# Attention scores by products over 64 rows and 72 keys, two heads side by side on the array, from keys kept unmasked in two copies

## The chip, the cores and the metric

The kernel runs on one core of one Trainium2 chip. The metric is the device time of one execution in microseconds (us). Of the kernel before there are three runs, with a median of 1661.16 us (1660.9 to 1661.81).

The engines of the core are called by the profile's names: PE (TensorE, matmuls), PEld (TensorE's weight loads, which the profile lists apart), DVE (VectorE), ACT (ScalarE), POOL (GpSimd) and SP (SyncE, which here issues most of the DMA transfers).

## The reference

Pooled attention is followed by two feed-forward layers. The change is in the attention, in the first product below.

```python
# q, k, v: (8, 8, 576, 64) f32
pool = 8
k_p = k.reshape(B, H, 72, pool, D).mean(axis=3)
v_p = v.reshape(B, H, 72, pool, D).mean(axis=3)
scores = 1 / sqrt(64) * q @ k_p^T            # (8, 8, 576, 72)
attn = exp(scores - max(scores)); attn /= attn.sum() + 1e-9
x = attn @ v_p                               # as 4608 tokens of 512
x = relu(x @ w_in) ** 2 @ w_out              # 512 -> 2048 -> 512
out = leaky(x @ w2_in) @ w2_out              # 512 -> 2048 -> 512
```

## The kernel before, in words

**Stages.** The first stage does the attention and the first product of the first feed-forward layer, `x @ w_in`, and stores the squares `h1`. `Middle` and `Second` then do the rest, with large products alone. The attention of block 0 (tokens 0 to 511) stands in `start()` in an order written out by hand (`START`), that of block 1 in `second_attention()`, and that of blocks 2 to 8 in a planner: `FirstStage` describes each step as an operation with an engine, a duration in us, a rank and buffers, and `Plan.run` sorts them by the times at which they could start. The program gets that order, engine by engine, and each engine then runs its own list strictly in order.

**Attention by tiles.** A tile is 128 tokens (36 tiles in 9 blocks of 512). A batch has 576 tokens, so four of the 36 tiles (4, 13, 22 and 31) belong half to one batch and half to the next (`parts_of`): there are 40 parts. For a tile the steps are: load q; four transposes on PE (line 682) and a copy by ACT (line 691) give `qt`, in which a pair of heads lies on the 128 partitions, head 2c on rows 0 to 63 and head 2c+1 on rows 64 to 127; the score products (line 728); the maximum of each head by DVE (line 738); the exponentials by ACT, one instruction for each head (line 750); the division (lines 767 to 769); the transposes of the probabilities (lines 808, 816); and their split into a high and a low part (lines 822, 825).

**Keys.** For each batch the 576 pooled keys (8 heads of 72) lie on partitions in five chunks of 128, the last of 64. `k_mask_parts` multiplies each pooled key row by a mask of two columns (1 for even and 0 for odd heads, and the reverse, times the scale), so that a row of 64 numbers becomes 128, of which one half is zero (line 524). Transposed (lines 550 and 556) they are `kt`, 128 by 576. With the zeros in place one product over 128 rows gives the scores of a pair of heads: 128 tokens by 144 keys, the first 72 columns of head 2c, the others of head 2c+1.

**Score products.** `score_parts(i, hf)` does half of a tile, two such products into one bank of PSUM; the planner places the two halves of a tile apart, with other work between. Each product in f32 appears in the trace as two weight loads and two matmul instructions.

**Rounding.** The large products of the stage (line 1000) are in f32r, one instruction each.

Of the kernel before, what the change touches and what calls it, by code (L numbers as in the profile page):

```python
# [16 lines left out]
P = 128  # L17
# [6 lines left out]
C_ID, C_PAR, C_VM, C_RA, C_RB, C_RP, C_N = 16, 0, 10, 12, 13, 14, 144  # L24


def constants(sp, nk, scale):
    c = np.zeros((P, C_N), np.float32)
    c[:, C_ID : C_ID + P] = np.eye(P, dtype=np.float32)
    p = np.arange(P)  # L30
    for t in range(nk):
        for j in range(2):
            c[:, C_PAR + 2 * t + j] = ((t * P + p) // sp % 2 == j) * (scale / POOL)
# [10 lines left out]
def attention_relu2_leaky_kernel(  # L44
# [26 lines left out]
    BLOCKS = NT // T  # L71

# [350 lines left out]
    kps, kts, kms, vps, vrps, vst, qT, sc = {}, {}, {}, {}, {}, {}, {}, {}  # L423
# [26 lines left out]

    def k_pool_pe(b, n):

        full, tail = KEYS // P, KEYS % P
        if n == 0:
            kps[b] = sb([P, 512], F32, "qt")[:, : NK * D].rearrange("p (c d) -> p c d", d=D)
            k_sums.extend([acc_bank(0), acc_bank(1)])
        ps, last = k_sums
        for c in range(2) if n == 0 else range(2, full):
            halves(ps, c, raws[("k", b, c)], P)
        if n == 0:  # L460
            return None
        halves(last, 0, raws[("k", b, full)], tail)

        def rest():
            halves_sum(kps[b][:, :full], ps, 0, full)
            halves_sum(kps[b][:tail, full:], last, 0, 1)

        return rest

    def k_pool(b, c):  # L470
        raw = raws[("k", b, c)]
        n = min(P, KEYS - c * P)
        if c == 0:
            kps[b] = sb([P, 512], F32, "qt")[:, : NK * D].rearrange("p (c d) -> p c d", d=D)
        nc.vector.tensor_reduce(
            out=kps[b][:n, c, :],
            in_=raw[:n].rearrange("p (r d) -> p d r", r=POOL),
            op=ALU.add,
            axis=AX.X,
        )  # L480

    def pooled_by_halves(out, x, n):

        def halve(w):
            to = out if w == D else x[:n, :, :w]
            nc.vector.tensor_tensor(
                out=to, in0=x[:n, :, :w], in1=x[:n, :, w : 2 * w], op=ALU.add
            )

        return [lambda w=w: halve(w) for w in (4 * D, 2 * D, D)]  # L490

    def k_pool_rows(b):
        kps[b] = sb([P, NK * D], F32, "kp").rearrange("p (c d) -> p c d", d=D)
        return pooled_by_halves(kps[b][:, : KEYS // P], raws.pop(("k", b, "rows")), P)

    def k_pool_tail(b):
        n = KEYS % P
        pooled_sum(kps[b][:n, KEYS // P], raws.pop(("k", b, "tail"))[:n])
# [9 lines left out]
    def k_mask(b):  # L508

        for fn in k_mask_parts(b):  # L510
            fn()

    def k_mask_parts(b):
        full, tail = KEYS // P, KEYS % P
        kp = kps.pop(b)
        km = (home() if b == 0 else sb([P, 512], F32, "r" if b == 1 else "gh"))[:, : full * 2 * D]
        km = km.rearrange("p (c j d) -> p c j d", j=2, d=D)
        kt = sb([P, 2 * D + 8], F32, "km")[:, : 2 * D].rearrange("p (j d) -> p j d", j=2)
        par = cst[:, C_PAR : C_PAR + 2 * NK].rearrange("p (c j) -> p c j", j=2)
        kms[b] = km, kt  # L520

        def masked(out, c0, c1, n):
            shape = [n, c1 - c0, 2, D]
# [7 lines left out]
        return [  # L531
            lambda: masked(km, 0, full, P),
            lambda: masked(kt.unsqueeze(1), full, NK, tail),
        ]
# [5 lines left out]
    def k_transpose_parts(b):  # L540
        full, tail = KEYS // P, KEYS % P
        km, last = kms.pop(b)
        copy = nc.vector.tensor_copy if b > 1 else nc.scalar.copy
        ps = {}

        def rows():
            kts[b] = sb([P, KEYS], F32, "kt")
            ps[0] = bank()
            for c in range(full):
                nc.tensor.transpose(  # L550
                    ps[0][:, c * P : (c + 1) * P], km[:, c].rearrange("p j d -> p (j d)"), ident
                )

        def rest():
            ps[1] = bank()
            nc.tensor.transpose(
                ps[1][:, :tail], last[:tail].rearrange("p j d -> p (j d)"), ident[:tail, :tail]
            )
# [138 lines left out]
    def score_products(i):  # L697
        rest = []
        for hf in range(2):
            products, top, exps = score_parts(i, hf)  # L700
            products()
            rest.append(lambda top=top, exps=exps: (top(), exps()))
        return rest

    def score_parts(i, hf):
        at = {}

        def products():
            if hf == 0:
                if i in first_tiles:  # L710
                    if not first_s:
                        t = home_tile([P, 3, KEYS]).rearrange("p n (h k) -> p n h k", h=H)
                        first_s.extend(t[:, n] for n in range(3))
                    s = first_s.pop()
                else:
                    s = sb([P, H, SP], F32, "s")
                sc[i] = s, sb([P, H], F32, "l"), sb([P, H], F32, "m"), qT.pop(i)
            qt = sc[i][3]
            if i in first_tiles:
                ps = acc_bank((2 * i + hf) % KC)  # L720
            else:
                ps = acc_bank(KC - 1) if i < 2 * T // P and hf == 0 else bank()
            at["ps"] = ps
            for b, _, r0, n in reversed(parts_of(i)):
                for c2 in range(NP // 2):
                    cc = hf * (NP // 2) + c2
                    keys = slice(cc * PAIR, (cc + 1) * PAIR)
                    nc.tensor.matmul(
                        ps[: r0 + n, c2 * PAIR : (c2 + 1) * PAIR],
                        lhsT=qt[:, cc, : r0 + n],  # L730
                        rhs=kts[b][:, keys],
                        start=True,
                        stop=True,
                    )

        def top():
            m = sc[i][2]
            nc.vector.tensor_reduce(  # L738
                out=m[:, hf * HH : (hf + 1) * HH],
                in_=at["ps"][:, : HH * SP].rearrange("p (h k) -> p h k", h=HH),  # L740
# [5 lines left out]
        def exps():  # L746
            s, l, m, _ = sc[i]
            for h in range(HH):
                g = hf * HH + h
                nc.scalar.activation(  # L750
                    out=s[:, g, :],
                    in_=at["ps"][:, h * SP : (h + 1) * SP],
# [5 lines left out]
        return products, top, exps  # L758
# [144 lines left out]
    def start():  # L903

        t0, rest, exps = 0, {}, {}
        for word in START:
# [21 lines left out]
            elif x == "k":  # L928
                for c in range(NK):
                    k_pool(n, c)  # L930
                k_mask(n)
# [129 lines left out]
    def second_attention():  # L1061
# [5 lines left out]
        pe[0] += [pooled_late[0], lambda: k_mask(b)]  # L1067
# [175 lines left out]
    class FirstStage:  # L1243
# [20 lines left out]
        def add_keys(self, b, rank):  # L1264
            rows, tail, kp, km, kl, kt = (
                Buffer(t) for t in ("wo4", "raw", "kp", "gh", "km", "kt")
            )
# [7 lines left out]
            for n, us in enumerate((1.22, 0.69, 0.43)):  # L1275
# [6 lines left out]
            y = self.op("DVE", 1.03, lambda: k_pool_tail(b), rank, after=[load_tail, x], uses=[tail, kp])  # L1282
            masks = []

            def mask(n):
                if n == 0:
                    masks.extend(k_mask_parts(b))
                masks[n]()
# [11 lines left out]
            t0 = self.op("PE", 0.63, lambda: turn(0), rank, after=[x, y], gets=[p0, kt], uses=[km])  # L1300
            c0 = self.op("DVE", 0.69, lambda: turn(1), self.CHAIN, after=[t0], uses=[p0, kt])
            t1 = self.op("PE", 0.2, lambda: turn(2), rank, after=[y, t0], gets=[p1], uses=[kl])
# [59 lines left out]
        def add_attention(self, blk):  # L1362
# [9 lines left out]
            for i in tiles:  # L1372
# [22 lines left out]
                for hf in range(2):  # L1395
# [4 lines left out]
                    self.tile[i] = x  # L1400
                    for b, *_ in parts_of(i):
                        self.scored[b] = x
                    after = [x]
# [893 lines left out]
```

## Time and profile before

| | us |
|---|---|
| median of three runs | 1661.16 |
| the profiled execution | 1660.31 |
| its span, first to last instruction | 1658.5 |
| PE busy in it | 1618.0 |
| DVE busy | 1264.1 |
| ACT busy | 834.4 |

The profiled execution lies 0.85 us under the median, and 1.8 us of it lie outside the span. Busy time is the union of an engine's instructions; the matmuls of PE overlap (the next begins before the last has drained), so its busy time says that something was under way, not that the array worked at its peak.

### The profile page before, as it was taken

The page shows a single profiled execution, that of the slowest core. Times are in us where ns is not written, and L with a number is a line of the kernel's source. Part 1 is how long each engine was busy: PE and PEld are TensorE (multiplying, and loading weights), DVE is VectorE, ACT ScalarE, POOL GpSimd, SP SyncE. Part 2 cuts the span into 40 slices and gives each one's busy share as a digit, 9 for nine tenths or more (in the row PEclk, how much of TensorE's full clock was granted, in tenths as well). Part 3 has the DMA queues.
Part 4 walks back from the last instruction along what each step waited for, and adds up shares of the span by engine and source line. Part 5 has one row for each costly group of instructions (what it writes and reads, how often), then busy time and mean ns, then how long its engine had stood idle before and what let it go on. Part 6 is the DMA issues. An engine that isn't in the chain of part 4 may idle for free. (4 is left out here: it accounts for less than half of the span.)

```text
span 1658.5 us, 26685 instructions
## 1 busy us (share of the span) xinstructions
PE 1618.0 (98%) x9560; PEld 1470.8 (89%) x9560; DVE 1264.1 (76%) x2214; ACT 834.4 (50%) x1797; POOL 102.4 (6%) x191
## 2 busy tenths in 40 slices
PE   7999889999999999999999999999999999999998
PEld 6888768888888898888888899999999999999998
DVE  7967879887766678696879887877877866666665
ACT  6766657756754754343435544443445533333332
POOL 0121011121121200000000000000000000000000
PEclk9999999999999999999999999999999999999999
DMA  8827766776566977575757766557638754544443
GB/s 236 268 89 221 221 213 218 228 247 218 189 229 217 330 241 258 186 251 189 253 206 249 281 212 211 181 191 235 204 131 291 242 169 153 159 154 153 153 156 106
DMA packets 272325, 345.78 MB, mean 208 GB/s; under 512 B 55360, under 2 KB 201024, under 8 KB 272192
## 3 DMA queue, kind: packets, MB, share of 16 engines
q1 hardware_dynamic: 257152, 296.36, 55.6%
q0 software_dynamic: 14464, 47.20, 7.6%
q8 instruction: 75, 1.23, 0.3%
q10 hardware_dynamic: 576, 0.52, 0.1%
q14 instruction: 58, 0.48, 0.1%
HBM read 208.74 MB, written 135.27 MB: 207 GB/s over the span
## 5 line engine op out<-in xcount | busy, mean ns | idle before, releaser
L1000 PE MATMUL acc<-xh,wi 128*128 128x512 f32 x640 | 221.3, 403 | 0.1
L1000 PE MATMUL acc<-wo,wi 128*128 128x512 f32 x704 | 191.2, 399 | 1.7 <-ACT r L1011 1.7
L1000 PEld LDWEIGHTS acc<-wo,wi 128*128 128x128 f32 x704 | 129.1, 188 | 27.4 <-ACT r L1011 2.0
L1000 PEld LDWEIGHTS acc<-xh,wi 128*128 128x128 f32 x640 | 121.2, 190 | 24.2 <-ACT r L1011 0.5
L1000 PE MATMUL acc<-xl,wi 128*128 128x512 f32 x320 | 125.6, 393 | 0.0
L2181 PE MATMUL ps<-wi,hh 128*128 128x256 f32 x512 | 93.9, 283 | 0.0
L2181 PE MATMUL acc<-wi,hh 128*128 128x256 f32 x496 | 91.1, 283 | 0.0
L2181 PE MATMUL ps<-wo,hh 128*128 128x256 f32 x496 | 90.9, 283 | 0.0
L2181 PE MATMUL acc<-wo,hh 128*128 128x256 f32 x484 | 88.9, 283 | 0.0
L1675 ACT CAST mh<-ms 128x512 fp32r<-128x512 f32 (+2 forms) x68 | 52.4, 771 | 70.3 <-DVE ms L1657 70.1
L750 ACT ACTIVATE s<-ps,m 128x72 f32<-128x72 f32 x240 | 74.1, 335 | 26.7 <-DVE m L738 26.5
L1938 PE MATMUL acc<-fh,wo 128*128 128x384 f32 x384 | 83.0, 338 | 2.9 <-DVE gh L1951 1.8
L1011 ACT ACTIVATE r<-acc 128x512 f32<-128x512 f32 x88 | 53.3, 607 | 63.4 <-PE acc L1000 55.6
L1938 PE MATMUL ps<-fh,wi 128*128 128x384 f32 x384 | 82.3, 336 | 0.7 <-DVE gh L1951 0.7
L1954 ACT ACTIVATE gh<-gh 128x384 f32<-128x384 f32 x48 | 25.3, 527 | 113.8 <-DVE gh L1951 113.8
L2181 PEld LDWEIGHTS ps<-wi,hh 128*128 128x128 f32 x512 | 79.9, 192 | 0.0
L2181 PEld LDWEIGHTS acc<-wi,hh 128*128 128x128 f32 x496 | 77.4, 192 | 0.0
L2181 PEld LDWEIGHTS ps<-wo,hh 128*128 128x128 f32 x496 | 77.4, 192 | 0.0
L1720 PE MATMUL acc<-mh,wi 128*128 128x512 f32 (+1 forms) x256 | 76.0, 362 | 0.0
L1720 PE MATMUL ps<-mh,wi 128*128 128x512 f32 (+1 forms) x256 | 76.0, 362 | 0.0
L2181 PEld LDWEIGHTS acc<-wo,hh 128*128 128x128 f32 x484 | 75.5, 192 | 0.0
L2181 PE MATMUL ps<-wi,hl 128*128 128x256 f32 x256 | 72.4, 283 | 0.0
(351 smaller groups left out, 4455.3 us busy)
## 6 DMA issues: line engine op xcount, KB each, us to landing
h<-r POOLq DMA_DIRECT2D x88, 256.0 KB, 4.3
hf<-r SPq DMA_DIRECT2D x96, 192.0 KB
ml<-h SPq DMA_DIRECT2D x34, 512.0 KB
ml<-h SPq DMA_DIRECT2D x60, 256.0 KB
hr<-hf SPq DMA_DIRECT2D x23, 640.0 KB
xl<-hf SPq DMA_DIRECT2D x23, 640.0 KB
xh<-hf SPq DMA_DIRECT2D x23, 640.0 KB
h<-st POOLq DMA_DIRECT2D x56, 256.0 KB, 4.0
```

Source lines behind the costliest of these rows:

```text
L750: nc.scalar.activation(out=s[:, g, :], in_=at["ps"][:, h * SP : (h + 1) * SP], func=AF.Exp, bias=m[:, g : g + 1], accum_out=l[:, g : g + 1],)
L1000: nc.tensor.matmul(acc_of[blk, c], lhsT=(wih, wil)[w][c][:, kc], rhs=xsplit[blk][x][kc], start=(kc, n) == order[0], stop=(kc, n) == order[-1],
L1011: nc.scalar.activation(out=r, in_=ps, func=AF.Relu)
L1675: nc.scalar.copy(hi[:, at], y)
L1720: nc.tensor.matmul(at[s][:, :n], lhsT=w[:, wx, b, s * P : (s + 1) * P], rhs=x[:, a], start=p == 0 and m == 0, stop=p == PAIRS - 1 and m == 2,)
L1938: nc.tensor.matmul(at, lhsT=w[:, FORMS[j], kc], rhs=x[j][:, kc], start=m == 0 and j not in (4, 6), stop=m == 5, skip_group_check=True,)
L1954: nc.scalar.activation(out=out_, in_=x, func=AF.Lrelu)
L2181: nc.tensor.matmul(at[:, s * TR : (s + 1) * TR], lhsT=x[:, a, s * P : (s + 1) * P], rhs=w[:, b], start=p == 0 and s == 0 and m == 0, stop= ...
```

## The change

The scores of a pair of heads are no longer one product over 128 rows and 144 columns with half of the keys zero, but two products over 64 rows and 72 columns: head 2c from rows 0 to 63, head 2c+1 from rows 64 to 127, into two different banks. So a tile takes 8 products where it took 4, all in one operation of the planner; bank j holds the four heads 2n+j. The keys need no mask: the pooled row is written twice, side by side, so that after the transposes both halves of the rows hold all keys, and the scale is applied in the copies of `kt` out of PSUM. For batches 2 to 7 the two copies come from the last step of the pooling itself, which writes with a broadcast. The buffers of the masked keys are gone, and the planner's numbers are adapted.

```diff
+    def key_sums():
+        return sb([P, NK, 2, D], F32, "kp")
...
     def k_pool_rows(b):
-        kps[b] = sb([P, NK * D], F32, "kp").rearrange("p (c d) -> p c d", d=D)
+        kps[b] = key_sums()
         return pooled_by_halves(kps[b][:, : KEYS // P], raws.pop(("k", b, "rows")), P)
...
-            nc.vector.tensor_tensor(
-                out=to, in0=x[:n, :, :w], in1=x[:n, :, w : 2 * w], op=ALU.add
-            )
+            to, a, b = x[:n, :, :w], x[:n, :, :w], x[:n, :, w : 2 * w]
+            if w == D:
+                to = out
+                if len(out.shape) > 3:
+                    a, b = (y.unsqueeze(2).to_broadcast(out.shape) for y in (a, b))
+            nc.vector.tensor_tensor(out=to, in0=a, in1=b, op=ALU.add)
...
-    def k_mask_parts(b):
+    def k_twice(b):
         full, tail = KEYS // P, KEYS % P
-            nc.vector.tensor_tensor(
-                out=out[:n],
-                in0=kp[:n, c0:c1, :].unsqueeze(2).to_broadcast(shape),
-                in1=par[:n, c0:c1, :].unsqueeze(3).to_broadcast(shape),
-                op=ALU.mult,
-            )
+        for x in (kps[b][:, :full], kps[b][:tail, full:]):
+            nc.vector.tensor_copy(x[:, :, 1], x[:, :, 0])
...
+        def copy(out, in_):
+            scaled(engine, out, in_, SCALE)
...
             for b, _, r0, n in reversed(parts_of(i)):
-                for c2 in range(NP // 2):
-                    cc = hf * (NP // 2) + c2
-                    keys = slice(cc * PAIR, (cc + 1) * PAIR)
-                    nc.tensor.matmul(
-                        ps[: r0 + n, c2 * PAIR : (c2 + 1) * PAIR],
-                        lhsT=qt[:, cc, : r0 + n],
-                        rhs=kts[b][:, keys],
+                for cc in range(NP):
+                    for j in range(2):
+                        rows, keys = slice(j * D, (j + 1) * D), (2 * cc + j) * SP
+                        nc.tensor.matmul(
+                            at[j][: r0 + n, cc * SP : (cc + 1) * SP],
+                            lhsT=qt[rows, cc, : r0 + n],
+                            rhs=kts[b][rows, keys : keys + SP],
...
-            for n, us in enumerate((1.22, 0.69, 0.43)):
+            for n, us in enumerate((1.22, 0.69, 0.69)):
...
-            x = self.op("DVE", 0.68, lambda: mask(0), rank, after=[x, y], gets=[km, kl], uses=[kp])
-            y = self.op("DVE", 0.28, lambda: mask(1), rank, after=[x, y], uses=[kp, kl])
...
-                for hf in range(2):
-                    products, top, ex = score_parts(i, hf)
-                    bank_ = Buffer("ps")
-                    x = self.op("PE", 0.65 * (1 + two), products, 2, after=after,
-                                gets=[bank_] + ([s, l, m] if hf == 0 else []), uses=[qt, *kts_])
+                products, halves_ = score_parts(i)
+                banks = Buffer("ps"), Buffer("ps")
+                x = self.op("PE", 0.9 * (1 + two), products, 2, after=after,
+                            gets=[*banks, s, l, m], uses=[qt, *kts_])
```

The order on PE at the very start, of the kernel before: the transposes of the first q tile and of the keys of batch 0, then the scores of tiles 0 and 1 (names: out<-in; `acc` is a bank, `kt` the keys, `wo` the buffer that holds `qt` here; partitions x columns).

```order
1 L682 MATMUL ps<-cst,wo_94 128x128 x4
2 L550 MATMUL ps<-cst,wo_147 128x128 x4
3 L556 MATMUL ps<-cst,km 128x64
4 L728 MATMUL acc_165<-kt,wo_106 128x144 x2
5 L728 MATMUL acc_168<-kt,wo_106 128x144 x2
6 L682 MATMUL ps<-cst,wo_94 128x128 x4
7 L728 MATMUL acc_192<-kt,wo_147 128x144 x2
8 L728 MATMUL acc_195<-kt,wo_147 128x144 x2
```

And of the change, up to the scores of tile 0:

```order
1 L663 MATMUL ps<-cst,wo_94 128x128 x4
2 L535 MATMUL ps<-cst,kp 128x128 x4
3 L539 MATMUL ps<-cst,kp 128x64
4 L706 MATMUL acc_163<-kt,wo_106 128x72
5 L706 MATMUL acc_164<-kt,wo_106 128x72
6 L706 MATMUL acc_163<-kt,wo_106 128x72
7 L706 MATMUL acc_164<-kt,wo_106 128x72
8 L706 MATMUL acc_163<-kt,wo_106 128x72
9 L706 MATMUL acc_164<-kt,wo_106 128x72
10 L706 MATMUL acc_163<-kt,wo_106 128x72
11 L706 MATMUL acc_164<-kt,wo_106 128x72
12 L663 MATMUL ps<-cst,wo_94 128x128 x4
```

The products go to the two banks in turn, so the first bank is whole only with the last but one, where it was whole after the second of four.

In the planned stretch, the order on PE of the kernel before around the two halves of one tile (line 1000 is the large product of the stage):

```order
733 L1000 MATMUL acc_2514<-xh,wi_1105 128x512
734 L1000 MATMUL acc_2569<-xh,wi_1105 128x512
735 L1000 MATMUL acc_2569<-xl,wi_1105 128x512
736 L1000 MATMUL acc_2569<-xh,wi_1105 128x512
737 L728 MATMUL ps<-kt,qt 128x144 x2
738 L1000 MATMUL acc_2508<-xh,wi_1062 128x512
739 L1000 MATMUL acc_2508<-xl,wi_1062 128x512
740 L1000 MATMUL acc_2508<-xh,wi_1062 128x512
741 L728 MATMUL ps<-kt,qt 128x144 x2
742 L1000 MATMUL acc_2514<-xh,wi_1105 128x512
```

And of the change around the scores of two tiles there (line 978 is the large product now):

```order
790 L706 MATMUL ps<-kt,qt 128x72 x8
791 L978 MATMUL acc_2620<-xh,wi_1138 128x512
792 L978 MATMUL acc_2620<-xl,wi_1138 128x512
793 L978 MATMUL acc_2620<-xh,wi_1138 128x512
794 L978 MATMUL acc_2612<-xh,wi_1138 128x512
795 L978 MATMUL acc_2612<-xl,wi_1138 128x512
796 L978 MATMUL acc_2612<-xh,wi_1138 128x512
797 L978 MATMUL acc_2672<-wo_2131,wi_298 128x512
798 L978 MATMUL acc_2672<-wo_2132,wi_298 128x512
799 L978 MATMUL acc_2672<-wo_2131,wi_298 128x512
800 L706 MATMUL ps<-kt,qt 128x72 x8
801 L978 MATMUL acc_2612<-xh,wi_1138 128x512
```

Both halves of a tile now stand together, so that PE goes from products over 128 rows to products over 64 and back once for each of the 36 tiles; the program has 320 score products in such 36 runs, where it had 160. The planner's order of the rest of blocks 2 to 8 differs throughout.

## Rows read from the trace of the kernel before

**Rows 1.** The page: busy time of the engines, and PE's busy tenths in 40 slices.

```profile
PE 1618.0 (98%) x9560; PEld 1470.8 (89%) x9560; DVE 1264.1 (76%) x2214; ACT 834.4 (50%) x1797; POOL 102.4 (6%) x191
...
PE   7999889999999999999999999999999999999998
```

**Rows 2.** Busy time of each engine by stretch of the span, granted clock, DMA.

```profile
core 0: us, PE busy (x) PEld busy (x) DVE busy (x) ACT busy (x) POOL busy (x), PEclk, DMA share, GB/s
0.00:40.00 40.00, 29.01 (x178) 26.27 (x179) 28.09 (x55) 24.85 (x94) 0.73 (x5) 1.00 0.82 231
40.00:130.00 90.00, 87.73 (x458) 73.10 (x457) 71.57 (x113) 61.19 (x169) 16.04 (x27) 1.00 0.55 181
130.00:500.00 370.00, 353.91 (x1837) 296.23 (x1837) 293.63 (x701) 242.73 (x788) 63.54 (x117) 0.98 0.69 221
```

**Rows 3.** The score products of line 728 alone, by stretch.

```profile
130.00:500.00 370.00, 41.42 (x240) 35.80 (x240) 0.98 0.69 221
...
sum 1658.00, PE 56.97 PEld 49.15; mean PE 14.24 PEld 12.29
```

**Rows 4.** What PE waited for between 130 and 500 us.

```profile
PE ps L682 <- DVE ptl L825: 8.3, 2, 7.9
PE ps L550 <- DVE gh L524: 2.7, 1, 2.7
PE ps L682 <- DVE xl L885: 1.7, 1, 1.7
PE acc L1000 <- ACT r L1011: 1.7, 1, 1.7
```

**Rows 5.** PE in order of time, one half of a tile's scores among large products.

```profile
231.66 0.66 PE L728 MATMUL ps<-kt,qt 128*128 128x144 f32 x4
232.05 0.49 PE L1000 MATMUL acc<-xh,wi 128*128 128x512 f32 x1
232.38 0.40 PE L1000 MATMUL acc<-xl,wi 128*128 128x512 f32 x1
232.61 0.62 PE L1000 MATMUL acc<-xh,wi 128*128 128x512 f32 x2
```

**Rows 6.** PE in order of time, products with only 64 moving columns.

```profile
78.56 0.28 PE L869 MATMUL ps<-pth,v_hi 128*128 128x64 f32 x1
78.67 0.28 PE L870 MATMUL ps<-pth,v_lo 128*128 128x64 f32 x1
78.79 0.28 PE L871 MATMUL ps<-ptl,v_hi 128*128 128x64 f32 x1
78.90 0.28 PE L872 MATMUL ps<-ptr,v_rem 96*128 96x64 f32 x1
```

**Rows 7.** PE around one transpose over 64 rows (line 556).

```profile
224.43 0.66 PE L728 MATMUL ps<-kt,qt 128*128 128x144 f32 x4
225.01 0.28 PE L556 MATMUL ps<-cst,km 64*128 64x64 f32 x1
225.22 0.50 PE L1000 MATMUL acc<-xh,wi 128*128 128x512 f32 x1
225.56 0.39 PE L1000 MATMUL acc<-xl,wi 128*128 128x512 f32 x1
```

**Rows 8.** PE at a split tile: four products of 128 tokens, four of 64.

```profile
185.35 1.29 PE L728 MATMUL ps<-kt,qt 128*128 128x144 f32 x8
186.58 0.66 PE L808 MATMUL ps<-cst,s 128*128 128x128 f32 x4
187.07 0.66 PE L728 MATMUL ps<-kt,qt 128*128 128x144 f32 x4
```

**Rows 9.** Weight loads by line and form: rows*columns, count, busy, mean ns.

```profile
L872 PEld LDWEIGHTS ps<-ptr,v_rem 96*128 96x128 f32 x64 | 12.5, 196 | 1.8 <-DVE ptr L825 1.0 <-issue 0.3
L871 PEld LDWEIGHTS ps<-ptl,v_hi 128*128 128x128 f32 x64 | 12.4, 194 | 0.5
...
L728 PEld LDWEIGHTS ps<-kt,qt 128*64 128x64 f32 x28 | 3.4, 148 | 1.2 <-issue 0.3
...
L432 PEld LDWEIGHTS ps<-gh,cst 128*128 128x128 f32 x8 | 1.0, 192 | 0.0
L432 PEld LDWEIGHTS acc<-raw,cst 64*64 64x64 f32 x8 | 0.8, 132 | 0.1
```

**Rows 10.** PE at the start, tiles 0 and 1.

```profile
12.14 2.29 PE L728 MATMUL acc<-kt,wo 128*128 128x144 f32 x8 [0.38 <-ACT kt L562]
14.22 1.06 PE L682 MATMUL ps<-cst,wo 128*128 128x128 f32 x4
15.96 2.29 PE L728 MATMUL acc<-kt,wo 128*128 128x144 f32 x8 [0.68 <-ACT wo L691]
```

**Rows 11.** Line 728 alone: count, duration in ns (min/median/max), starts, forms.

```profile
L728 PE MATMUL acc<-kt,wo x32: 286/447/609, 12.1 to 24.9; 128*128 128x144 f32 x32
```

**Rows 12.** DVE there and later: the masks, and an operation on 128x256.

```profile
9.62 0.67 DVE L524 TENSOR_TENSOR wo<-qt,cst 128x512 f32<-128x512 f32 x1
10.22 0.28 DVE L524 TENSOR_TENSOR km<-qt,cst 64x128 f32<-64x128 f32 x1
...
33.37 0.30 DVE L618 TENSOR_SCALAR vh<-vp 128x256 fp32r<-128x256 f32 x1
```

**Rows 13.** The longest stall: DVE, then PE.

```profile
244.16 0.43 DVE L408 TENSOR_TENSOR wo<-gl 128x256 f32<-128x256 f32 x1 [9.40 <-DMA w1o<-wo]
...
246.94 1.12 PE L682 MATMUL ps<-cst,raw 128*128 128x128 f32 x4 [7.92 <-DVE ptl L825]
```

More of the change, by code (lines that the diff above doesn't have):

```diff
@@ L30, in constants @@
     p = np.arange(P)
-    for t in range(nk):
-        for j in range(2):
-            c[:, C_PAR + 2 * t + j] = ((t * P + p) // sp % 2 == j) * (scale / POOL)
     c[:, C_VM] = p < sp
@@ L464, in rest @@
         def rest():
-            halves_sum(kps[b][:, :full], ps, 0, full)
-            halves_sum(kps[b][:tail, full:], last, 0, 1)
+            halves_sum(kps[b][:, :full, 0], ps, 0, full)
+            halves_sum(kps[b][:tail, full:, 0], last, 0, 1)
         return rest
@@ L473, in k_pool @@
         if c == 0:
-            kps[b] = sb([P, 512], F32, "qt")[:, : NK * D].rearrange("p (c d) -> p c d", d=D)
+            kps[b] = key_sums()
         nc.vector.tensor_reduce(
-            out=kps[b][:n, c, :],
+            out=kps[b][:n, c, 0],
             in_=raw[:n].rearrange("p (r d) -> p d r", r=POOL),
@@ L484, in halve @@
         def halve(w):
-            to = out if w == D else x[:n, :, :w]
-            nc.vector.tensor_tensor(
-                out=to, in0=x[:n, :, :w], in1=x[:n, :, w : 2 * w], op=ALU.add
-            )
+            to, a, b = x[:n, :, :w], x[:n, :, :w], x[:n, :, w : 2 * w]
[4 more added lines that the diff above has]
+            nc.vector.tensor_tensor(out=to, in0=a, in1=b, op=ALU.add)
         return [lambda w=w: halve(w) for w in (4 * D, 2 * D, D)]
     def k_pool_rows(b):
-        kps[b] = sb([P, NK * D], F32, "kp").rearrange("p (c d) -> p c d", d=D)
+        kps[b] = key_sums()
         return pooled_by_halves(kps[b][:, : KEYS // P], raws.pop(("k", b, "rows")), P)
@@ L497, in k_pool_tail @@
         n = KEYS % P
-        pooled_sum(kps[b][:n, KEYS // P], raws.pop(("k", b, "tail"))[:n])
+        to = kps[b][:n, KEYS // P]
+        pooled_sum(to[:, 0], raws.pop(("k", b, "tail"))[:n])
+        nc.vector.tensor_copy(to[:, 1], to[:, 0])
     def v_pool_rows(b):
@@ L541, in k_transpose_parts @@
         full, tail = KEYS // P, KEYS % P
-        km, last = kms.pop(b)
-        copy = nc.vector.tensor_copy if b > 1 else nc.scalar.copy
+        kp = kps.pop(b).rearrange("p c j d -> p c (j d)")
+        engine = nc.vector if b > 1 else nc.scalar
         ps = {}
+        def copy(out, in_):
+            scaled(engine, out, in_, SCALE)
         def rows():
@@ L549, in rows @@
             for c in range(full):
-                nc.tensor.transpose(
-                    ps[0][:, c * P : (c + 1) * P], km[:, c].rearrange("p j d -> p (j d)"), ident
-                )
+                nc.tensor.transpose(ps[0][:, c * P : (c + 1) * P], kp[:, c], ident)
         def rest():
             ps[1] = bank()
-            nc.tensor.transpose(
-                ps[1][:, :tail], last[:tail].rearrange("p j d -> p (j d)"), ident[:tail, :tail]
-            )
+            nc.tensor.transpose(ps[1][:, :tail], kp[:tail, full], ident[:tail, :tail])
         return [
@@ L697, in score_products, with score_parts @@
     def score_products(i):
-        rest = []
-        for hf in range(2):
[L700 to L706, printed above, removed]
-        def products():
-            if hf == 0:
+        products, halves_ = score_parts(i)
+        products()
+        return [lambda top=top, exps=exps: (top(), exps()) for top, exps in halves_]
+    def score_parts(i):
+        at = []
+        def products():
+            if i in first_tiles:
+                if not first_s:
+                    t = home_tile([P, 3, KEYS]).rearrange("p n (h k) -> p n h k", h=H)
+                    first_s.extend(t[:, n] for n in range(3))
+                s = first_s.pop()
+            else:
+                s = sb([P, H, SP], F32, "s")
+            qt = qT.pop(i)
+            sc[i] = s, sb([P, H], F32, "l"), sb([P, H], F32, "m")
+            for j in range(2):
@@ L710, in products @@
                 if i in first_tiles:
[L711 to L714, printed above, removed]
-                else:
[L716 to L722, printed above, removed]
@@ L736, in top @@
-        def top():
-            m = sc[i][2]
+                    at.append(acc_bank((2 * i + j) % KC))
+                else:
+                    at.append(acc_bank(KC - 1) if i < 2 * T // P and j == 0 else bank())
+            for b, _, r0, n in reversed(parts_of(i)):
+                for cc in range(NP):
+                    for j in range(2):
+                        rows, keys = slice(j * D, (j + 1) * D), (2 * cc + j) * SP
[3 more added lines that the diff above has]
+                            rhs=kts[b][rows, keys : keys + SP],
+                            start=True,
+                            stop=True,
+                        )
@@ L738, in top @@
+        def top(j):
+            m = sc[i][2].rearrange("p (n j) -> p j n", j=2)
             nc.vector.tensor_reduce(
-                out=m[:, hf * HH : (hf + 1) * HH],
-                in_=at["ps"][:, : HH * SP].rearrange("p (h k) -> p h k", h=HH),
+                out=m[:, j],
+                in_=at[j][:, : HH * SP].rearrange("p (h k) -> p h k", h=HH),
                 op=ALU.max,
@@ L744, in top, with exps @@
             )
[L746 to L749, printed above, removed]
+        def exps(j):
+            s, l, m = sc[i]
+            for n in range(HH):
+                g = 2 * n + j
                 nc.scalar.activation(
                     out=s[:, g, :],
-                    in_=at["ps"][:, h * SP : (h + 1) * SP],
+                    in_=at[j][:, n * SP : (n + 1) * SP],
                     func=AF.Exp,
@@ L756, in exps @@
                 )
-        return products, top, exps
+        return products, [(lambda j=j: top(j), lambda j=j: exps(j)) for j in range(2)]
     def normalize(i):
@@ L1264, in add_keys @@
         def add_keys(self, b, rank):
-            rows, tail, kp, km, kl, kt = (
-                Buffer(t) for t in ("wo4", "raw", "kp", "gh", "km", "kt")
-            )
+            rows, tail, kp, kt = (Buffer(t) for t in ("wo4", "raw", "kp", "kt"))
             load = self.dma(
@@ L1281, in add_keys @@
                 x = self.op("DVE", us, fn, rank, after=after, gets=[kp] if n == 0 else (), uses=[rows, kp])
[L1282 to L1288, printed above, removed]
-            x = self.op("DVE", 0.68, lambda: mask(0), rank, after=[x, y], gets=[km, kl], uses=[kp])
-            y = self.op("DVE", 0.28, lambda: mask(1), rank, after=[x, y], uses=[kp, kl])
+            y = self.op("DVE", 1.2, lambda: k_pool_tail(b), rank, after=[load_tail, x], uses=[tail, kp])
             parts = []
@@ L1299, in add_keys @@
             p0, p1 = Buffer("ps"), Buffer("ps")
-            t0 = self.op("PE", 0.63, lambda: turn(0), rank, after=[x, y], gets=[p0, kt], uses=[km])
+            t0 = self.op("PE", 0.63, lambda: turn(0), rank, after=[x, y], gets=[p0, kt], uses=[kp])
             c0 = self.op("DVE", 0.69, lambda: turn(1), self.CHAIN, after=[t0], uses=[p0, kt])
-            t1 = self.op("PE", 0.2, lambda: turn(2), rank, after=[y, t0], gets=[p1], uses=[kl])
+            t1 = self.op("PE", 0.2, lambda: turn(2), rank, after=[y, t0], gets=[p1], uses=[kp])
             c1 = self.op("DVE", 0.22, lambda: turn(3), self.CHAIN, after=[t1, c0], uses=[p1, kt])
@@ L1394, in add_attention @@
                 exps = []
-                for hf in range(2):
-                    products, top, ex = score_parts(i, hf)
-                    bank_ = Buffer("ps")
-                    x = self.op("PE", 0.65 * (1 + two), products, 2, after=after,
-                                gets=[bank_] + ([s, l, m] if hf == 0 else []), uses=[qt, *kts_])
[L1400 to L1403, printed above, removed]
+                products, halves_ = score_parts(i)
+                banks = Buffer("ps"), Buffer("ps")
+                x = self.op("PE", 0.9 * (1 + two), products, 2, after=after,
+                            gets=[*banks, s, l, m], uses=[qt, *kts_])
+                self.tile[i] = x
+                for b, *_ in parts_of(i):
+                    self.scored[b] = x
+                for bank_, (top, ex) in zip(banks, halves_):
                     y = self.op("DVE", 0.46, top, self.CHAIN, after=[x], uses=[bank_, m])
```

29 lines of the change are left out of this document (5 added, 24 removed).

## The prediction

> **What bounds the kernel now.** The page says PE: busy for 98% of the span, DVE for 76%, ACT for 50% [rows 1]. A kernel whose bound is PE in the mean may have stages with another bound, so I read the busy times by stretch next. The score products all lie before 500 us [rows 3], and three quarters of them (240 of 320 instructions) between 130 and 500 us, where PE is under way for 353.9 of 370 us [rows 2]; DVE, with 293.6, is not far behind. The list of what PE waited for there adds up to about 17 us, and half of it is one stall of 7.9 us [rows 4]. So between 40 and 500 us a microsecond more on PE is, to a first approximation, a microsecond more in the end, and one less is one less. The first 40 us are different: PE idles or runs slowly for a chain through ACT and DVE, and what counts there is when a bank is whole.
>
> **What a score product costs now.** One half of a tile is four instructions. From its start at 231.66 to that of the second large product at 232.38 are 0.72 us [rows 5]; one large product takes 0.23 (232.38 to 232.61), so the four take 0.49, 0.122 each. A tile of one part has eight: **0.98 us**, with every weight load hidden under the instruction before it. (The busy sum of 57 us [rows 3] is more than 320 times 0.122 = 39 us, since the drain of the last one and the slow start are in it.)
>
> **What a load costs.** Products with 64 moving columns follow each other in 0.11 us [rows 6], though by the 0.23 for 512 columns the moving alone would be 0.03. What is left is the loading of 128 columns of weights: **0.11 us, a floor under each instruction that needs a new load**. It goes by columns: loads of 64x64 last 132 ns where 128x128 last 192, which is 0.06 less for 64 columns fewer; loads of 96 rows last 196 where those of 128 rows last 194 [rows 9], so fewer rows gain nothing. The Trainium skill, "TensorE: Matmul & The Clock Gate", section "LDWEIGHTS (loading the stationary operand)", says the same: time by columns, not by the rows contracted. By that rule a product over half of the rows has no shorter load, which speaks against this change, and no run shows a 64x128 load of this kind yet.
>
> **What a change of shape costs.** In [rows 7] a 64-row transpose stands between products over 128 rows. The last score instruction starts at 224.43 + 3 x 0.122 = 224.80; the transpose starts 0.21 later (0.09 over the 0.122), the next product 0.21 after it, and the second 0.34 after that, where 0.23 is usual: its load was not hidden (0.11). From 224.43 to 225.56 are 1.13 us; without change of shape it would be 4 x 0.122 + 0.11 + 0.23 = 0.83. One trip to 64 rows and back costs 0.30. [rows 8] give it a second time, for 64 columns in place of 64 rows: the eight take 1.23 to the next start instead of 0.98, and the four behind them 0.49, for an estimated 0.44 (four times 0.11). The array drains for about 0.09 on the way in and on the way out, and the first load on either side lies bare. The Trainium skill, "TensorEngine Tiling (Array Packing)", section "Key Properties", says that a change of tiling mode drains the engine; by that rule, the trace agrees, with 0.21 in place of 0.122.
>
> **The new part, step by step.** Sixteen instructions, each with a load of 128 columns (0.11) and 72 moving columns (half of 144: 0.061). The order is: first head high and low, second head high and low. Each half of the rows must load 8 times, so 8 x 0.11 = 0.88 is the least for loads by columns. Both ends of what the trace doesn't show, whether loads into the two halves overlap: all in a row, 16 x 0.11 = 1.76; in pairs as the order allows (the second load of one half goes beside the first of the other), nine rounds, 0.99. I take the pairs: the halves share no row, and a load already runs beside a product. With 0.09 in, 0.99 of rounds, 0.06 for the last product, 0.09 out and 0.11 of bare load: **1.34 for 0.98, +0.36 a tile.**
>
> **The sum.** Tiles 4 to 35 are 28 whole and 4 split ones. Whole: 28 x 0.36 = +10.1. Split before: two halves of 0.98 + 0.30, 2.56. After: 0.09 + 0.99 + 0.06, then a change of shape (0.09) and a 64-column load (0.055), eight rounds set by the 0.061 of the product (0.49), 0.06, and 0.20 out: 2.03. That is 4 x -0.53 = -2.1. Tiles 0 to 3: two starts are 3.82 apart (15.96 - 12.14), since PE waits for ACT's copy, which stands behind the exponentials of the first bank [rows 10]. The eight take 2.29; less the 0.447 of the last one [rows 11] that is 1.84, or seven steps of 0.24 and a bare load of 0.16. The step is twice 0.122, as at 1.2 instead of 2.4 GHz, though the clock column says 1.00 there [rows 2]. The first bank was whole after 0.16 + 4 x 0.24 = 1.12; now after eight rounds of 0.16 and one product, 1.40: +0.3 for each of four tiles, with 0.1 added for the second bank, +1.6. Ahead of them go the two masks (0.67 + 0.28), and two copies come, by a 128x256 operation of 0.30 and half of it [rows 12]: -0.5. Start: +1.1. In all 10.1 - 2.1 + 1.1 = **+9.1** on 1660.3, so 1669.4, and with the 0.85 by which this execution lies under the median, **1670**.
>
> **What I cost at nothing.** DVE loses two masks a batch (0.95) and gains about 0.26 in the last pooling step and a small copy; it waits between 130 and 500 us for a fifth of the time [rows 2], and its relief helps only where PE waits for it. One such wait is for a mask itself, 2.7 us [rows 4]; I let it stand against the later first bank of each tile. ACT does as many exponentials as before. The scale in the copies of the keys changes no copy's size. Two banks of four are taken at once, and a tile's maxima come up to 1 us later; behind them on DVE and ACT stand the splits of other tiles, for which PE waits once they hold its banks. The cover is the large products between. If it is gone, each tile pays up to that 1 us.
>
> **The new order.** The planner sorts everything anew. The long stall began with DVE, which waited 9.4 us for the landing of a store; PE found no free bank until 246.94 [rows 13]. It may vanish or come elsewhere: 0 by choice, -11 (7.9 and the slow products behind it) to +10 as bounds.
>
> **The rivals.**
> - *Loads in a row* (one loader for both halves). For it: every load in the trace starts after the one before it has begun its product. 0.09 + 1.76 + 0.06 + 0.20 = 2.11 a tile, +1.13: 28 x 1.13 = 31.6; split tiles 3.2 for 2.56, +2.7; start 16 x 0.16 instead of 1.12, +1.3 for each of four less 0.5, +4.7. Sum +39: **1700**. Then the two halves don't work side by side, and the change doesn't do what it says.
> - *Faster: half the rows load in half the time*, or under each other entirely, so that the products set the pace, 8 x 0.061 = 0.49 a tile. Then 0.09 + 0.11 + 0.49 + 0.20 = 0.89, -0.09: 28 x -0.09 = -2.5; split tiles 1.5 for 2.56, -4.1; start -0.9. Sum -7.5: **1653**. It decides from rounds under 0.07 us; [rows 9] speak against it with 96 rows, and 64 have not been seen. The Trainium skill, "TensorEngine Tiling (Array Packing)", section "Theoretical Speedup", has up to twice the speed for 64 rows; without drains that would be an estimate of 40 parts x 0.49, -20.
> - *Faster by the order*: the stall of [rows 13] and most of the others in [rows 4] go, -16 against +9: **1654**.
> - *Slower by the order*: a further stall like it, +10: **1680**.
>
> **Chances.** Pairs 0.45, loads in a row 0.2, products set the pace 0.15, faster by the order 0.08, slower by it 0.12. 0.2% is 3.3 us, about what a measurement tells from no change. Pairs and both slower cases give slower, less a few hundredths where the order takes back some 6 us (same); the two faster ones give faster, with a little for their upper ends: faster 0.2, same 0.08, slower 0.72. The likeliest case alone spans 1663 to 1678. The range takes in most of both neighbours, 1655 to 1703.
>
> **What would show it.** Right: between two score products on the two halves, starts 0.055 apart in the mean, about 1.0 from the first to the last of a tile, 0.2 before the first and 0.34 to the second large product behind them. Starts 0.11 apart would be loads in a row, 0.03 the products' pace. PE's waits between 130 and 500 us should stay near 17 us. Wrong: no gap at the changes of shape, or stalls of DVE that grow or vanish by more than 10 us.

## The result, and the profile after

The changed kernel takes 1677.47 us (median of four, 1676.73 to 1681.33) where the kernel before takes 1661.49 beside it: a ratio of 1.0098, interval 1.0083 to 1.0113, 16.0 us slower. The forecast was slower, 1670, from 1655 to 1703. Two disturbed executions beside the experiments (1771.97 us of the kernel before, 5467.02 in experiment 5) count in the medians given below, but not in the ratios.

The page of the changed kernel, as [rows 1]:

```profile
PE 1623.8 (97%) x9880; PEld 1469.0 (88%) x9880; DVE 1261.4 (75%) x2208; ACT 837.1 (50%) x1797; POOL 103.2 (6%) x191
...
PE   7999799999999979999999999999999999999998
```

PE is busy for 5.8 us more in a span that is 16.6 us longer, so it also stands idle for longer. Of its 40 slices two weak ones (7) tell where: the fifth, where the kernel before has an 8, and the fifteenth, from 586 to 628 us, where it has a 9.

One tile's scores in the changed kernel, PE in order of time (line 706 is the score product, 978 the large one):

```profile
257.78 0.84 PE L978 MATMUL acc<-wo,wi 128*128 128x512 f32 x3
258.55 1.11 PE L706 MATMUL ps<-kt,qt 64*128 64x72 f32 x16
259.60 0.50 PE L978 MATMUL acc<-xh,wi 128*128 128x512 f32 x1
259.94 0.39 PE L978 MATMUL acc<-xl,wi 128*128 128x512 f32 x1
```

The weight loads of those score products (PEld; in brackets how long the first waited, and for what):

```profile
258.55 0.97 PEld L706 LDWEIGHTS ps<-kt,qt 64*128 64x128 f32 x16 [0.35 <-DVE m L716]
```

The last of the three large products starts at 257.78 + 2 x 0.227 = 258.23. The first score product follows 0.32 later instead of 0.23: 0.09 of drain. (The wait that the load's row puts down to DVE doesn't explain it: behind a large product nearly every tile from 120 to 500 us shows the same 0.32 to 0.33.) All sixteen are over at 259.66, and from 259.60 to the second large product there are 0.34 instead of 0.23: the bare load, 0.11. From 258.55 to 259.60 are 1.05, and with 0.09 and 0.11 the tile costs **1.25 us** of PE for 0.98, +0.27. Sixteen loads of 128 columns began within 0.97 less the 0.19 of the last, 0.78: in seven steps of 0.11, two loads to a step. So the two halves of the rows load and multiply side by side, the first pair of loads too.

What PE waited for between 130 and 520 us, as [rows 4]:

```profile
PE ps L663 <- DVE l L745: 9.4, 1, 9.4
PE ps L706 <- DVE ptr L803: 4.0, 1, 4.0
PE ps L794 <- DVE ptl L803: 3.7, 1, 3.7
```

That list is little longer than the one before: 18.5 us in all for 15.9, with the long stall now at 188 us. The start of the second stage is another matter. In the kernel before PE passes into it without idling, and waits 2.36 us nine us later (line 1000 is the first stage's large product there, 1720 the second stage's):

```profile
583.91 0.39 PE L1000 MATMUL acc<-xh,wi 128*128 128x512 f32 x1
584.13 0.28 PE L1720 MATMUL ps<-mh,wo 128*128 128x256 f32 x1
...
593.12 0.38 PE L1720 MATMUL ps<-mh,wo 128*128 128x256 f32 x1 [2.36 <-ACT mh L1675]
```

In the changed kernel PE, and ACT beside it, in order of time:

```profile
592.57 0.39 PE L978 MATMUL acc<-xh,wi 128*128 128x512 f32 x1
602.88 0.58 PE L1686 MATMUL ps<-mh,wo 128*128 128x256 f32 x1 [9.93 <-ACT wo L1659]
```

```profile
602.00 0.83 ACT L1659 CAST wo<-wo 128x768 fp32r<-128x768 f32 x1 [5.46 <-DMA wo<-w1o]
```

PE is idle for 9.9 us; ACT waits for the landing of the first weights of the second stage. SP's list says why they come late:

```profile
593.93 0.37 SPq L408 DMA_DIRECT2D w2o<-wo  x1
594.39 0.52 SPq L1653 DMA_DIRECT2D wi<-w1o  x1
594.97 2.33 SPq L1653 DMA_DIRECT2D wo<-w1o  x3
```

They are issued at 594.97, behind the last store of the weight forms that the first stage makes on DVE in idle moments, and into buffers that these forms used. The last subtractions of those forms (line 406, count, ns, first and last start) run in the changed kernel until 593.6, in the kernel before (line 408) until 553.0:

```profile
L406 DVE TENSOR_TENSOR wo<-gl,wo x44: 291/292/294, 199.2 to 593.6; 128x128 f32<-128x128 f32 x44
```

```profile
L408 DVE TENSOR_TENSOR wo<-gl,wo x44: 291/292/294, 179.1 to 553.0; 128x128 f32<-128x128 f32 x44
```

Nothing in the change touches these forms. The planner put them 40 us later; it sorts everything by times that the change altered.

So the 16.6 us can be followed along the span (starts of PE's instructions, us; the last row is the changed kernel with its old products, experiment 1):

| | first large product | last one of the first stage | first of the second stage | first of the last stage | end |
|---|---|---|---|---|---|
| before | 40.87 | 583.91 | 584.13 | 935.2 | 1658.5 |
| changed | 43.65 | 592.57 | 602.88 | 951.6 | 1675.1 |
| difference | +2.8 | +8.7 | +18.8 | +16.4 | +16.6 |
| experiment 1 | 40.17 | 582.70 | 593.28 | 941.7 | 1664.3 |

Up to the end of the first stage the change costs 8.7, the passage to the second 10.1 more, and 2.4 come back there, where the wait of 2.36 is gone.

At the start two tiles stand 4.36 us apart (11.24 to 15.60), 3.82 before [rows 10]; ACT's q copy waits behind the exponentials of a bank that is whole later:

```profile
11.24 1.98 PE L706 MATMUL acc<-kt,wo 64*128 64x72 f32 x16 [0.39 <-ACT kt L597]
13.15 1.12 PE L663 MATMUL ps<-cst,wo 128*128 128x128 f32 x4
15.60 1.99 PE L706 MATMUL acc<-kt,wo 64*128 64x72 f32 x16 [1.33 <-ACT wo L672]
```

The first score product comes 0.9 us earlier (11.24 for 12.14); 0.5 of that is an earlier landing of the first q (8.62 for 9.12). The first large product comes later:

```profile
43.65 0.40 PE L978 MATMUL acc<-xh,wi 128*128 128x512 f32 x1
```

In the kernel before it is at 40.87. Most of these 2.8 us don't come from the products' own work. In the kernel before the long steps of the start end before tile 3; in the changed one tile 3 and part of the 32 transposes behind it still go by them:

```profile
24.30 1.99 PE L706 MATMUL acc<-kt,wo 64*128 64x72 f32 x16
26.22 5.36 PE L430 MATMUL ps<-wo,cst 128*128 128x128 f32 x32
```

```profile
23.99 1.15 PE L728 MATMUL acc<-kt,wo 128*128 128x144 f32 x8
24.98 3.73 PE L432 MATMUL ps<-wo,cst 128*128 128x128 f32 x32
```

### The profile page after: what moved, and what is told of

Same layout as the page of the kernel before. It is cut to its first block, busy times and chain, and to the rows that moved or that the text cites. A ratio compares the mean times of both kernels' runs of the same rounds, so it can differ in the third digit from the quotient of the medians.

```text
span 1675.1 us, 27311 instructions
## 1 busy us (share of the span) xinstructions
PE 1623.8 (97%) x9880; PEld 1469.0 (88%) x9880; DVE 1261.4 (75%) x2208; ACT 837.1 (50%) x1797; POOL 103.2 (6%) x191
## 5 line engine op out<-in xcount | busy, mean ns | idle before, releaser
L1686 PE MATMUL ps<-mh,wo 128*128 128x512 f32 (+1 forms) x224 | 68.1, 365 | 10.1 <-ACT wo L1659 9.9
```

The lines of the kernel that those rows point to most:

```text
L1686: nc.tensor.matmul(at[s][:, :n], lhsT=w[:, wx, b, s * P : (s + 1) * P], rhs=x[:, a], start=p == 0 and m == 0, stop=p == PAIRS - 1 and m == 2,)
```

## The experiments

Theory A: the products and changes of shape cost the 16 us. Theory B: they cost about 7.6, and the rest comes from where the new order puts the stalls. Each ratio is to the kernel before on the same chip.

**1. The products alone undone.** The order of all other instructions is that of the changed kernel.

```diff
                 for cc in range(NP):
-                    for j in range(2):
-                        rows, keys = slice(j * D, (j + 1) * D), (2 * cc + j) * SP
-                        nc.tensor.matmul(
-                            at[j][: r0 + n, cc * SP : (cc + 1) * SP],
-                            lhsT=qt[rows, cc, : r0 + n],
-                            rhs=kts[b][rows, keys : keys + SP],
+                    c2 = cc % 2
+                    nc.tensor.matmul(
+                        at[cc // 2][: r0 + n, c2 * PAIR : (c2 + 1) * PAIR],
+                        lhsT=qt[:, cc, : r0 + n],
+                        rhs=kts[b][:, cc * PAIR : (cc + 1) * PAIR],
```

> The changed kernel with the score products over 128 rows and 144 columns again (four to a tile, both banks filled by one planned operation); every other instruction stands in the order of the changed kernel. The keys are unmasked, so a product adds the scores of both heads of a pair: the separation of the heads is left out. Theory A (the array: the products over 64 rows and the changes of shape cost nearly all of the 16 us): 1661 to 1663. Theory B (the products cost about 7.6 us, 28 tiles x 0.27 less 4 x 0.67 and 2.7 at the start, and the new order the rest): 1668 to 1671, with the stall at the start of the second stage still 7 us or more.

Measured: 1668.49 for 1660.49, ratio 1.0046 (1.0028 to 1.0064): +8.0 with the old products, +16.0 with the new ones. The products cost 8.0 us (by the two intervals an estimate of 8 with some 4 to either side) and what is left, the order and the unmasked keys, another 8.0. Its waits from 130 to 620 us:

```profile
PE ps L1685 <- ACT wo L1658: 10.2, 1, 10.2
PE ps L663 <- DVE l L744: 9.5, 1, 9.5
PE ps L705 <- DVE ptr L802: 4.3, 1, 4.3
```

All three long stalls of the changed kernel are there without a single score product over 64 rows, so they belong to the order. PE at the end of its first stage:

```profile
582.70 0.39 PE L977 MATMUL acc<-xh,wi 128*128 128x512 f32 x1
593.28 0.58 PE L1685 MATMUL ps<-mh,wo 128*128 128x256 f32 x1 [10.19 <-ACT wo L1658]
```

To the end of the first stage the same order with the old products is 1.2 us ahead of the kernel before (582.70 for 583.91), and 9.9 ahead of the changed kernel: so far the order, with the unmasked keys and the halves of a tile in one place, costs nothing, and the products 9.9 by these traces. What the order costs comes at the passage to the second stage, 10.6 (593.28 - 582.70) for 0.2. The first large product starts early:

```profile
40.17 0.40 PE L977 MATMUL acc<-xh,wi 128*128 128x512 f32 x1
```

Against it the products cost 3.5 us at the start (43.65 - 40.17). That is one pair of executions. From PE's first instruction to the first large product the changed kernel takes 35.03; the same start takes 32.65, 32.65, 32.91, 34.54 and 35.38 in the traces of experiments 2, 4, 10, 9 and 8, since its long steps end sooner or later. With the old products it is 31.41 here, 31.75 in the kernel before and 29.64 in experiment 6. The means, 33.9 and 30.9, are 2.9 apart. A gain from leaving out the masks is not shown.

**2. The planner's number made true.**

```diff
-                x = self.op("PE", 0.9 * (1 + two), products, 2, after=after,
+                x = self.op("PE", 1.25 * (1 + two), products, 2, after=after,
```

> The changed kernel with one number of the planner changed: a tile's score products are put at 1.25 us, what the trace shows them to take, not at 0.9. Theory A: as the changed kernel, 1676 to 1679. Theory B: the stall of 9.9 us at the start of the second stage falls to 3 or less, since the loads of its first weights stand earlier among the stored forms in SP's list: 1667 to 1672.

Measured: 1667.73 for 1660.49, ratio 1.0047 (1.0029 to 1.0065). Its waits from 130 to 620 us:

```profile
PE ps L663 <- DVE xl L863: 5.1, 1, 5.1
PE ps L535 <- DVE ptr L803: 4.7, 3, 3.2
PE ps L1686 <- ACT mh L1641: 2.8, 1, 2.8
```

The stall of 9.9 is gone: PE passes into the second stage without idling (585.15), and the 2.8 come later, as the 2.36 in the kernel before. The last subtraction of a stored form starts at 553.7. As theory B had it. What remains, +7.2, is near the price of the products, but the four executions lie far apart (1662.53 to 1670.05), and the traced one, the fastest, has a span only 2.3 longer than the kernel before (1660.8 for 1658.5); all its waits from 130 to 620 us add up to 16.0, those of the kernel before to 18.6. It is one of the two best orders of the changed kernel found (the other is in experiment 10), and by the median slower than the kernel before.

**3. The heads apart.**

```diff
-                for cc in range(NP):
-                    for j in range(2):
+                for j in range(2):
+                    for cc in range(NP):
```

> The changed kernel with the products of the even heads first, then those of the odd ones, so that neighbours are on the same half of the rows. If the two halves load and multiply side by side only when they stand in turn: 16 steps of 0.11 instead of eight, +0.8 a tile on 32 tiles and +1.2 on the first four, +28 to +33, 1704 to 1711. If the engine finds the overlap itself: 1677.

Measured: 1695.76 for 1660.49, ratio 1.0209 (1.0194 to 1.0224), +35.3: 19 over the changed kernel, less than the 28 to 33 expected. One tile in it:

```profile
266.27 1.62 PE L706 MATMUL ps<-kt,qt 64*128 64x72 f32 x16
267.82 0.50 PE L978 MATMUL acc<-xh,wi 128*128 128x512 f32 x1
```

From the first to the next large product are 1.55, not the 1.05 in turn, nor the 1.76 and drain of a pure row. So side by side they run when they stand in turn; in this order the trace shows part of them overlapping where the first head's end meets the second head's start.

**4. Fewer stored forms early.**

```diff
-    STORED_EARLY = 38
+    STORED_EARLY = 34
```

> The changed kernel with 34 instead of 38 of the stored weight forms made in the first stage; the other four are made later, behind the second stage's products. Theory B with the stored forms as the cause of the stall at the start of the second stage: the stall falls from 9.9 to 3 us or less, 1669 to 1673. Theory A, or a stall with another cause: 1676 to 1679.

Measured: 1691.85 for 1660.49, ratio 1.019 (1.0172 to 1.0208), a miss: +31.4, some 15 us more than the changed kernel. Its waits from 590 to 1300 us:

```profile
PE ps L1904 <- ACT gh L1924: 12.0, 1, 12.0
PE acc L1904 <- DVE gh L1917: 6.2, 4, 4.0
PE ps L1686 <- ACT mh L1641: 3.8, 1, 3.8
```

The stall at the start of the second stage is gone (PE's first product there starts at 591.09, 11.8 earlier), and 3.8 us come later in it. But in the last stage a new one of 12.0 and one of 4.0 came, where ACT waits for the words of a form made there:

```profile
1250.49 0.65 ACT L241 ACTIVATE val<-val 128x512 f32<-128x512 f32 x1 [7.20 <-DMA val<-in_moe_w_out]
```

So, as experiment 2 shows too, the late forms were the cause of the first stall, and moving four of them out of the first stage only moved the wait.

**5 and 6. The kernel before with another number.** No product is changed.

```diff
-                    x = self.op("PE", 0.65 * (1 + two), products, 2, after=after,
+                    x = self.op("PE", 0.49 * (1 + two), products, 2, after=after,
```

> The kernel before with one number of the planner changed: a half of a tile's scores at 0.49 us, what its four instructions occupy PE for, not at 0.65. No instruction is added or taken away, only the order changes. Theory B (the order alone moves several us, by where the stalls fall): outside 1661 by 3 to 10 us, either way, with the difference in PE's stalls between 130 and 600 us. Rival (the order hardly matters, so that the rest of the 16 us has another cause): 1659 to 1663.

Measured: 1671.02 for 1660.91, ratio 1.006 (1.0041 to 1.0079): +10 by the order alone. The same kernel once more, for its trace:

> The kernel before with 0.49 us for a half of a tile's scores once more, for its trace: theory B says that its 10 us stand as idle time of PE, one or two stalls of 5 us or more between 130 and 600 us that the kernel before has not, while its score products step by 0.122 as ever; rival: no such stall, and the time lies in slower steps.

It took 1669.46 us for 1660.65, in a single run. Its waits from 130 to 620 us:

```profile
PE ps L816 <- DVE ptl L825: 6.1, 1, 6.1
PE ps L682 <- issue: 5.4, 1, 5.4
PE ps L728 <- DVE xl L885: 2.7, 1, 2.7
```

Two stalls of over 5 us, as expected, where the kernel before has one of 7.9 [rows 4]; the list is longer too. The time stands as idle time of PE: behind its first instruction PE idles for 39.9 us (1667.7 - 1618.5 - 9.3) where it was 31.4 (1658.5 - 1618.0 - 9.1), 8.5 of the 9.2 by which the span is longer. Its score products step as before: four of them take 0.39 to the start of the next large product in both.

**7. Over all rows, 72 columns.** The order is that of the changed kernel.

```diff
-                            lhsT=qt[rows, cc, : r0 + n],
-                            rhs=kts[b][rows, keys : keys + SP],
+                            lhsT=qt[:, cc, : r0 + n],
+                            rhs=kts[b][:, keys : keys + SP],
```

> The changed kernel with its eight products to a tile over all 128 rows, still with 72 columns each and into two banks in turn; the order is that of the changed kernel. Each product adds the scores of both heads: the separation of the heads is left out. No change of shape, but no second half to load beside. If a load of 128 columns is the floor of each instruction: 16 x 0.11 = 1.76 a tile for 1.25, with the split tiles and the start +23, 1697 to 1704. If the moving columns set the pace: 16 x 0.061 = 0.98, about the 1668 of the run with 144 columns.

Measured: 1696.82 for 1660.91, ratio 1.0214 (1.0191 to 1.0237), just under the range expected. One tile:

```profile
267.42 1.90 PE L706 MATMUL ps<-kt,qt 128*128 128x72 f32 x16
269.12 0.48 PE L978 MATMUL acc<-xh,wi 128*128 128x512 f32 x1
```

With 0.275 for the last one, fifteen steps take 1.62: 0.108 each, the floor of the load, though 72 columns move in 0.061. So the products of the change are not cheap by their size; what they gain over this is the second half loading beside the first.

**8 to 10. Other numbers for the changed kernel,** 1.1, 1.4 and 1.2 in the line of experiment 2.

> The changed kernel with the planner's number for a tile's products at 1.1 us. Theory B: between 1664 and 1680, by the stalls of its own order; the part of the products stays (some 9 us over an order with the stalls of before). Theory A: 1676 to 1679.

> The changed kernel with the planner's number for a tile's products at 1.4 us, above what they take. Theory B: between 1664 and 1680, as with 1.1; the loads of the second stage's first weights early in SP's list, and no stall over 5 us at its start. Theory A: 1676 to 1679.

> The changed kernel with 1.2 us for a tile's products, next to the 1.25 that gave 1668. If an honest number makes a good order: 1665 to 1671. If the order is luck: anywhere from 1664 to 1681, as 1.1 (1675) and 1.4 (1677) were.

Measured: 1674.87 for 1660.91, ratio 1.0081 (1.0059 to 1.0103); 1676.59 for 1660.91, ratio 1.0098 (1.007 to 1.0126); and 1668.92 for 1660.65, ratio 1.0044 (1.0026 to 1.0063). With 0.9 and 1.25, that makes five orders of the changed kernel with 38 forms stored early: two lie 7 to 8 us above the kernel before (1.2 and 1.25), three 14 to 16 (0.9, 1.1 and 1.4). The 1674.87 lies in theory B's range alone; the 1676.59 lies in both and decides nothing. The long stalls sit elsewhere each time; with 1.4, as PE's waits from 230 to 400 us say, in the middle of the first stage, and the longest at the start of the second is 3.0, as expected:

```profile
PE ps L794 <- DVE ptr L803: 11.4, 2, 6.0
PE ps L535 <- DVE ptr L803: 4.3, 1, 4.3
```

By the medians no order tried made the changed kernel as fast as the kernel before. The two numbers near what the products take gave the best two; five tries don't show that this is a rule.

## Why the prediction was right in sign and small in size

**Pairs: right.** The two halves load side by side. Experiments 3 and 7 take the pairs away and cost 19 and 20 us over the changed kernel. The rounds were eight, not nine: the first pair of loads starts together too, so a tile costs 1.25 and not 1.34.

**Changes of shape: right.** 0.09 in, 0.09 out and 0.11 for the bare load were forecast; the rows give 0.09, 0.09 (0.20 from the last product to the next load, of which 0.11 is usual) and 0.11. Tile for tile the term was +0.36 and is +0.27.

**Split tiles:** forecast at 2.03 for 2.56. A split tile takes 32 instructions in one trip; below it the same tile with the old products (experiment 1):

```profile
276.75 1.76 PE L706 MATMUL ps<-kt,qt 64*128 64x72 f32 x32
278.44 0.73 PE L978 MATMUL acc<-wo,wi 128*128 128x512 f32 x2
```

```profile
269.53 2.27 PE L705 MATMUL ps<-kt,qt 128*128 128x144 f32 x16
271.73 0.98 PE L977 MATMUL acc<-wo,wi 128*128 128x512 f32 x3
```

1.69 to the next product, with 0.09 and 0.11 1.89: 0.14 a tile better than forecast. The old products in one place take 2.20, with 0.11 2.31, so 0.25 of the gain over 2.56 comes from putting the halves together.

**The start: mis-sized.** +1.1 was forecast, 43.65 - 40.87 = +2.8 it is. The first two steps from tile to tile grew by 0.54, not by 0.4, the third by 0.14. What the sum left out is that the long steps last into tile 3 (0.93 more to the next instruction) and the 32 transposes (1.63 more); how far they last differs from execution to execution.

**The products in all** were put at 10.1 - 2.1 + 1.6 = 9.6 without the gain from the masks. By the rows they are 28 x 0.27 + 4 x (1.89 - 2.31) + 3.5 = 9.4, where 2.31 is a split tile's price with the old products in one place; by experiment 1 against the changed kernel, 8.0 in the medians and 9.9 to the end of the first stage in the traces.

**The step that failed is the new order, put at "0 by choice".** It cost 8.0 (experiment 1), inside the bounds of -11 to +10. Among the scores the choice was good: the long stall of [rows 13] vanished and two of 9.4 and 4 us came, nearly a draw, and with its order the first stage ends 1.2 us sooner than in the kernel before (experiment 1). But 9.9 us of idle time came at 593 us, behind the scores: the rival "slower by the order", with a chance of 0.12, by another wait than the one it names. I had read [rows 4], 15.9 us and not about 17, only to 500 us, where the scores end. The planner's list runs on to the second stage's first weights. That 1677.47 still lies at the upper edge of the likeliest case's 1663 to 1678 is owed to the width of that range; the 1670 itself was right only for the products.

**Faster rivals:** the products' own pace (0.03 between starts in the mean) did not come; loads of 128 columns stay at 0.11 for 64 rows. **Loads in a row** did not either.

**What stays open:** why the planner put the stored forms 40 us later with 0.9 and not with 1.25 was not traced through its choices; and how much of the time in each order is due to the lower clock behind a stall (the granted clock, between its levels of 1.2 and 2.4 GHz, is 0.68 of the upper one from 600 to 610 us in the changed kernel, behind the idle 9.9 us, and 1.00 there in the kernel before).

## What to carry to other kernels

Count weight loads before columns: a product that is halved in rows and columns keeps its load. With the second half of the rows loading beside it the sixteen took 1.05 us here where they took 1.70 without (experiment 7), which only comes near the eight old ones; each trip to another shape of the array cost about 0.3 us on top, so gather such products into few trips. Where a planner orders the work by numbers, hold the order fixed when measuring an edit (experiment 1): its share was as large as that of the edit. And read such an order to the end of its list, for work done in idle moments can be late exactly where the next stage waits for it.

## What the runs showed of the hardware

Two weight loads into the two halves of the rows begin within one step, and products over 64 rows then come in twos every 0.11 us. At the start, where steps are twice as long, a round takes 0.2 and the clock column still says 1.00 (0 to 40 us, as in [rows 2]); how long that lasts moved the first large product of one and the same start by up to 2.7 us. And the same program's order alone, with not one instruction more, moved the kernel before by 10 us (experiment 5).
